# Running TensorE as two 64-row tiles in a two-problem attention kernel, with a planned load order

## The chip, the cores and the metric

The kernel runs on one core of a Trainium2 chip. The metric is the device time of one execution in microseconds (us), given as the median of several executions. A profiled execution comes with each kernel; its span differs from the median by a microsecond or two.

Engines in the profile: PE is TensorE's matmuls and PEld its weight loads, DVE is VectorE, ACT is ScalarE, POOL is GpSimd, SP is SyncE, which issues the DMAs.

## The reference

Two independent attention problems, A and B, of the same shape; the outputs are put side by side.

```python
B, Sq, D = 16, 144, 448
H, Sk, Dh = 16, 512, 256

def problem(x, k_cache, v_cache, wq, wo):            # all bf16
    q = (x @ wq).reshape(B, Sq, H, Dh).transpose(0, 2, 1, 3)
    scores = einsum("bhqd,bhkd->bhqk", q, k_cache) * Dh ** -0.5
    p = softmax(scores, axis=-1)
    o = einsum("bhqk,bhkd->bhqd", p, v_cache)
    return o.transpose(0, 2, 1, 3).reshape(B, Sq, H * Dh) @ wo

out = concatenate([problem(A...), problem(B...)], axis=-1)
```

A "unit" below is one (problem, batch, head), so there are 2 x 16 x 16 = 512. Each unit needs its own 512 x 256 K and V. For units 0 to 47 K is loaded as it lies and transposed on TensorE; from unit 48 on (464 units) the DMA transposes it. D is 448 = 3.5 x 128: this half is what the change is about.

## The kernel before

Per unit, PE does Q (8 matmuls with 128 contraction rows; the fourth chunk of D holds only 64 real rows and 64 zero rows), scores (8 matmuls of 144 columns), PV (8), a row sum (one matmul against a matrix of ones, for two units at a time), and on average 2.27 matmuls of 448 columns of the output projection. Q is done for two batches at once where it can be, in matmuls of 288 columns.

```python
wq_sb = sb("wq_sb", [128, 4, H * DH], BF16)      # fourth chunk: rows 0-63 set to zero
...
def t_q(U):
    ...
    def e(t):
        for dc in range(2):
            for kc in range(4):                  # 4 chunks of 128 rows: 3.5 are data
                c0 = h * DH + dc * 128
                acc = qp_ps[:, dc, 0:2 * SQ] if n == 2 else qp_ps[:, 0, dc * SQ:(dc + 1) * SQ]
                ins = t.matmul(acc, lhsT=wq_sb[:, kc, c0:c0 + 128],
                               rhs=xt_sb[:, kc, xo:xe + 1:max(xe - xo, 1), :], start=(kc == 0), stop=(kc == 3))
        return ins
...
def t_pv(U):
    ...
    ob = U % 2                                   # two PSUM banks for PV, by turns
    def e(t):
        for dc in range(2):
            for c in range(4):
                ins = t.matmul(ot_ps[ob][:, dc * SQ:(dc + 1) * SQ],
                               lhsT=v_sb[:, vsl, j, c * DH + dc * 128:c * DH + (dc + 1) * 128],
                               rhs=pt_sb[:, sl, c, :], start=(c == 0), stop=(c == 3))
        return ins
...
def t_halves(U):                                 # DVE: folds the exponentials' sums to 64 rows
    sl, p0 = U // 2 % NPS, U % 2 * 64            # two units share the 128 rows of one tile
    def e(v):
        return v.tensor_tensor(ps_sb[p0:p0 + 64, sl, :], p2_sb[0:64, :], p2_sb[64:128, :], op=ALU.add)
```

ACT takes the logarithm of the row sum and then exp(-log) for the reciprocal. DVE multiplies PV by it into a ring buffer (the "eviction") and, for every second unit, takes the maximum and minimum of the row sums; a flag computed from these selects a slow general path if a sum is out of bounds (it never is in these runs). The row sums start on POOL (`t_presum`), are folded on DVE (`t_halves`), and end in the matmul with ones.

The order of each engine's instructions is fixed when the kernel is built, and each engine runs them strictly in order:

```python
while True:
    ...
    for u in of_step(lq, i):
        if q_pair(u):
            t_q(u); t_evac_q(u)
    for u in of_step(ls, i):
        t_s(u)
    ...
    if P0 <= u < NT and u % 2:
        t_recip(u)
    if 0 <= u < NT:
        t_pv(u)
        if u < P0 or u % 2 == 0:
            t_sum(u)
    if P0 <= u + 2 < NT:
        t_halves(u + 2)                          # two units ahead
    ...
```

All eight PSUM banks are used: three for scores, two for Q, two for PV with the row sum, one for the projection. The loads follow two hand-written tables, one at the start and one at the switch from problem A to B.

## Time and profile before

| | before |
|---|---|
| median (2 runs) | 1055.65 us (1055.01 to 1056.3) |
| span of the profiled run | 1055.3 us |
| PV of unit 48 / of unit 511 begins | 126.4 us / 1045.1 us |
| PE busy | 98% |

The first view is the profile's page: span, busy times, the PE row of the 40 slices (busy tenths), the DMA queues (packets, MB, share of 16 engines), and the chain of work that ended last.

```profile
span 1055.3 us, 32320 instructions
PE 1031.0 (98%) x12376; PEld 875.0 (83%) x12376; DVE 740.9 (70%) x2039; ACT 793.9 (75%) x2365; POOL 636.6 (60%) x1030
...
PE   6999999999999999999999899999999999999997
...
q1 hardware_dynamic: 588896, 291.99, 110.9%
q8 instruction: 99, 1.62, 0.6%
...
PE 91%; DMA 5%; ACT 1%; DVE 1%; SPq 1%; issue 0%; POOL 0%; ACTq 0%; DVEq 0%
```

TensorE bounds the kernel: it is busy nearly throughout and is 91% of the chain. The line that looks like nothing is `q8 instruction`: 99 packets of 16 KB, the fetches of instructions. By the Trainium skill (cited below) one such packet is 256 instructions.

The timeline of PE near 500 us (start, us, engine, line, operation, count) shows that columns alone set the pace: eight matmuls of 144 columns begin every 0.50 us, 63 ns each, although one lasts about 230 ns.

```profile
500.05 0.66 PE L1142 MATMUL ot_ps<-pt_sb,v_sb 128*128 128x144 bf16 x8
500.55 0.23 PE L1158 MATMUL ot_ps<-ps_sb,ones 128*128 128x144 bf16 x1
500.61 0.54 PE L1259 MATMUL op_ps<-wo_sb,ring 128*128 128x448 bf16 x2
500.99 0.66 PE L1052 MATMUL qp_ps<-xt_sb,wq_sb 128*128 128x144 bf16 x8
501.49 0.66 PE L1086 MATMUL s_ps<-qt_sb,kt_sb 128*128 128x144 bf16 x8
```

The waits of PE (what it waited for: us in total, times, longest) are all small, and the two long ones after unit 48 are DMA waits at the switch from A to B.

```profile
PE s_ps L1000 <- DMA v_sb<-in_A_k_cache_dram: 6.3, 4, 4.7
PE qp_ps L1052 <- DMA wq_sb<-in_B_wq_dram: 3.6, 1, 3.6
PE s_ps L1086 <- DMA kt_sb<-in_B_k_cache_dram: 2.9, 1, 2.9
...
PE s_ps L1086 <- DVE qt_sb L1066: 1.5, 5, 0.4
```

The halving on DVE (busy us, mean ns, then idle before it):

```profile
L1120 DVE TENSOR_TENSOR ps_sb<-p_sb 64x144 bf16<-64x144 f32 x464 | 158.7, 342 | 44.4 <-POOL p_sb L1111 30.3
```

### The profile page before, as it was taken

The page shows a single profiled execution, that of the slowest core. Times are in us where ns is not written, and L with a number is a line of the kernel's source. Part 1 is how long each engine was busy: PE and PEld are TensorE (multiplying, and loading weights), DVE is VectorE, ACT ScalarE, POOL GpSimd, SP SyncE. Part 2 cuts the span into 40 slices and gives each one's busy share as a digit, 9 for nine tenths or more (in the row PEclk, how much of TensorE's full clock was granted, in tenths as well). Part 3 has the DMA queues.
Part 4 walks back from the last instruction along what each step waited for, and adds up shares of the span by engine and source line. Part 5 has one row for each costly group of instructions (what it writes and reads, how often), then busy time and mean ns, then how long its engine had stood idle before and what let it go on. Part 6 is the DMA issues. An engine that isn't in the chain of part 4 may idle for free.

```text
span 1055.3 us, 32320 instructions
## 1 busy us (share of the span) xinstructions
PE 1031.0 (98%) x12376; PEld 875.0 (83%) x12376; DVE 740.9 (70%) x2039; ACT 793.9 (75%) x2365; POOL 636.6 (60%) x1030
## 2 busy tenths in 40 slices
PE   6999999999999999999999899999999999999997
PEld 6999888888888888888878788888888888888885
DVE  4776666776766777777868667677776667777775
ACT  4887667777777777878857667777877777788785
POOL 3554556656666566666746556566666666666673
PEclk9999999999999999999999999999999999999999
DMA  9999999999999999999999999999999999999960
GB/s 316 372 343 291 294 291 248 283 299 271 264 305 260 248 286 262 304 289 280 283 281 343 279 283 287 303 284 292 251 279 280 278 286 298 296 254 274 292 201 14
DMA packets 589060, 294.15 MB, mean 279 GB/s; under 512 B 500832, under 2 KB 513632, under 8 KB 588896
## 3 DMA queue, kind: packets, MB, share of 16 engines
q1 hardware_dynamic: 588896, 291.99, 110.9%
q8 instruction: 99, 1.62, 0.6%
q14 instruction: 65, 0.53, 0.2%
HBM read 161.48 MB, written 4.13 MB: 157 GB/s over the span
## 4 chain that ended last, share of the span: by engine, by line
PE 91%; DMA 5%; ACT 1%; DVE 1%; SPq 1%; issue 0%; POOL 0%; ACTq 0%; DVEq 0%
PE s_ps L1086 23%; PE ot_ps L1142 23%; PE qp_ps L1052 22%; PE op_ps L1259 19%; DMA kt_sb<-in_B_k_cache_dram 2%; DMA v_sb<-in_A_k_cache_dram 2%; PE ot_ps L1158 2%; PE s_ps L1000 1%; PE qp_ps L1000 1%; DMA wq_sb<-in_B_wq_dram 1%; PE qp_ps L1259 1%; ACT rinv_sb L1179 0%; ACT pt_sb L1096 0%; DVE ring L1194 0%; DVE qt_sb L1066 0%
## 5 line engine op out<-in xcount | busy, mean ns | idle before, releaser
L1106 POOL TENSOR_TENSOR pp_sb<-pt_sb 128x288 f32<-128x288 bf16 x512 | 384.9, 752 | 322.5 <-ACT pt_sb L1096 308.1
L1096 ACT ACTIVATE pt_sb<-s_ps 128x288 bf16<-128x288 f32 x1024 | 364.6, 408 | 184.4 <-PE s_ps L1086 177.6
L1194 DVE TENSOR_TENSOR ring<-ot_ps,rinv_sb 128x288 bf16<-128x288 f32 (+2 forms) x640 | 241.9, 394 | 150.3 <-ACT rinv_sb L1179 145.8
L1086 PE MATMUL s_ps<-qt_sb,kt_sb 128*128 128x144 bf16 x4096 | 341.3, 226 | 4.7 <-DMA kt_sb<-in_B_k_cache_dram 2.9
L1142 PE MATMUL ot_ps<-pt_sb,v_sb 128*128 128x144 bf16 x4096 | 340.3, 226 | 0.0
L1086 PEld LDWEIGHTS s_ps<-qt_sb,kt_sb 128*128 128x128 bf16 x4096 | 287.7, 98 | 56.9 <-DVE qt_sb L1066 5.6
L1179 ACT ACTIVATE rinv_sb<-ln_sb 64x144 f32<-64x144 f32 x928 | 298.3, 321 | 24.3
L1052 PE MATMUL qp_ps<-xt_sb,wq_sb 128*128 128x288 bf16 (+1 forms) x2368 | 302.3, 271 | 6.6 <-DMA wq_sb<-in_B_wq_dram 3.6
L1259 PE MATMUL op_ps<-wo_sb,ring 128*128 128x448 bf16 x1120 | 285.2, 353 | 0.0
L1052 PEld LDWEIGHTS qp_ps<-xt_sb,wq_sb 128*128 128x128 bf16 x2368 | 212.3, 98 | 81.9 <-issue 7.5
L1142 PEld LDWEIGHTS ot_ps<-pt_sb,v_sb 128*128 128x128 bf16 x4096 | 274.5, 98 | 0.5
L1111 POOL TENSOR_TENSOR p_sb<-pp_sb 128x144 f32<-128x144 f32 x464 | 227.5, 490 | 74.6 <-DVE ps_sb L1120 10.4
L1209 DVE TENSOR_REDUCE run_sb<-ot_ps 128x1 bf16<-128x144 f32 x560 | 146.5, 304 | 79.4 <-ACT ln_sb L1166 44.3
L1120 DVE TENSOR_TENSOR ps_sb<-p_sb 64x144 bf16<-64x144 f32 x464 | 158.7, 342 | 44.4 <-POOL p_sb L1111 30.3
L1066 DVE CAST qt_sb<-qp_ps 128x576 bf16<-128x576 f32 x216 | 162.1, 751 | 21.3 <-PE qp_ps L1052 17.7
L1259 PEld LDWEIGHTS op_ps<-wo_sb,ring 128*128 128x128 bf16 x1120 | 94.0, 98 | 21.2
L1166 ACT ACTIVATE ln_sb<-ot_ps 128x144 f32<-128x144 f32 x232 | 67.9, 293 | 32.6 <-PE ot_ps L1158 25.3
L1158 PE MATMUL ot_ps<-ps_sb,ones 128*128 128x144 bf16 x280 | 63.4, 226 | 0.0
L1065 DVE CAST qt_sb<-qp_ps 128x288 bf16<-128x288 f32 x80 | 35.9, 448 | 4.8 <-PE qp_ps L1052 4.3
L1008 ACT ACTIVATE kt_sb<-qp_ps 128x512 bf16<-128x512 bf16 x48 | 28.9, 603 | 7.3 <-PE qp_ps L1000 7.3
L1111 POOL TENSOR_TENSOR ps_sb<-pp_sb 128x144 bf16<-128x144 f32 x48 | 23.5, 490 | 6.9 <-PE ot_ps L1158 0.3
L1158 PEld LDWEIGHTS ot_ps<-ps_sb,ones 128*128 128x128 bf16 x280 | 27.5, 98 | 0.0
(29 smaller groups left out, 153.4 us busy)
## 6 DMA issues: line engine op xcount, KB each, us to landing
v_sb<-in_A_v_cache_dram SPq DMA_DIRECT2D x128, 512.0 KB, 7.1
v_sb<-in_B_v_cache_dram SPq DMA_DIRECT2D x128, 512.0 KB, 7.5
v_sb<-in_A_k_cache_dram SPq DMA_DIRECT2D x24, 512.0 KB, 9.6
out_dram<-ost_sb SPq DMA_DIRECT2D x36, 112.0 KB, 6.2
wo_sb<-in_A_wo_dram SPq DMA_DIRECT2D x8, 448.0 KB, 8.7
wo_sb<-in_B_wo_dram SPq DMA_DIRECT2D x8, 448.0 KB, 9.0
wq_sb<-in_A_wq_dram SPq DMA_DIRECT2D x4, 768.0 KB, 10.1
wq_sb<-in_B_wq_dram SPq DMA_DIRECT2D x4, 768.0 KB, 10.6
```

Of the source, the lines that this page charges most:

```text
L1052: ins = t.matmul(acc, lhsT=wq_sb[:, kc, c0:c0 + 128], rhs=xt_sb[:, kc, xo:xe + 1:max(xe - xo, 1), :], start=(kc == 0), stop=(kc == 3))
L1066: return v.tensor_copy(qt_sb[:, a:b + 1:b - a, :, :], qp_ps[:, :, 0:2 * SQ].rearrange("p e (u q) -> p u e q", u=2))
L1086: ins = t.matmul(s_ps[bank][:, (c % 2) * SQ:(c % 2 + 1) * SQ], lhsT=kt_sb[:, 2 * c + dc, ko:ko + 128], rhs=qt_sb[:, qsl, dc, :], start=(dc ...
L1096: return a.activation(pt_sb[:, psl, 2 * k:2 * k + 2, :].rearrange("p b q -> p (b q)"), s_ps[bank][:, 0:2 * SQ], AF.Exp, scale=DH ** -0.5)
L1106: return g.tensor_tensor(pp_sb[:, :, :], pt_sb[:, psl, 0:2, :], pt_sb[:, psl, 2:4, :], op=ALU.add)
L1111: return g.tensor_tensor(dst, pp_sb[:, 0, :], pp_sb[:, 1, :], op=ALU.add)
L1120: return v.tensor_tensor(ps_sb[p0:p0 + 64, sl, :], p2_sb[0:64, :], p2_sb[64:128, :], op=ALU.add)
L1142: ins = t.matmul(ot_ps[ob][:, dc * SQ:(dc + 1) * SQ], lhsT=v_sb[:, vsl, j, c * DH + dc * 128:c * DH + (dc + 1) * 128], rhs=pt_sb[:, sl, c, ...
L1179: return a.activation(rinv_sb[p0:p0 + 64, sl, :], ln_sb[h0:h0 + 64, :], AF.Exp, scale=-1.0)
L1194: ins = v.tensor_tensor(ring[:, 2 * h:2 * h + 2, r0:r0 + q1 - q0], ot_ps[ob][:, 0:2 * SQ].rearrange("p (c q) -> p c q", c=2)[:, :, q0:q1], ...
L1209: return v.tensor_reduce(run_sb[:, k, j:j + 1], ot_ps[ob][:, 2 * SQ:3 * SQ], axis=AX.X, op=op)
L1259: ins = t.matmul(acc[0:m, 0:D], lhsT=ring[:, c, col0:col0 + m], rhs=wo_sb[:, c, :], start=(c == first), stop=(c == last))
```

## The change

The intent: since 448 = 7 x 64, Q needs only seven half-chunks of contraction instead of eight. If PE is used as two tiles of 64 rows that run side by side, every matmul becomes two halves with half the rows each, both adding into the same PSUM bank, and Q's two output halves need 7 half-matmuls each, 14 in place of 16. That removes one eighth of Q. Two tiles may not write one bank at once (the prediction names the page that says so), so the upper tile runs one group behind the lower.

With it come: an extra copy of x's last 64 rows to the other half of the partitions (DVE); the row sum as one half-matmul per unit (before: one whole one per two units); log and reciprocal done whole for each unit on ACT; the max and min checks replaced by running sums that the halving and the reciprocal write on the side; deeper buffers for Q (13 for 11) and for the partial row sums (2 for 1); and a planner that orders the loads from estimated times. The diff, cut to its core:

```diff
+    def tiles(self, lo, hi, after=None, clear=(), rank=1, **kw):
+        own = set(kw["banks"]) | set(clear)
+        ...                                       # upper groups on the same banks go first
+        self._put(PL, lo, self._ready((lo, after, kw)), **kw)      # lower tile now
+        self.late.append((hi, after, kw, self.step, rank))         # upper tile later
+        while self.late:
+            k, first = self._next()
+            if first > self.now[PL]:
+                break
+            self._pop(k)
...
-        wq_sb = sb("wq_sb", [128, 4, H * DH], BF16)
+        wq_sb = sb("wq_sb", [128, 3, H * DH], BF16)
+        wr_sb = sb("wr_sb", [128, H * 128], BF16)                  # last 64 rows, one half per dc
...
+        def q_tiles(U, dc):
+            ...
+            def tile(p):                          # p is LO (rows 0-63) or HI (64-127)
+                ms = [mm(acc, wq_sb[p, kc, c0:c0 + 128], xt_sb[p, kc, xsl, :], n * SQ, p is LO and kc == 0)
+                      for kc in range(3)]
+                if (p is HI) == (dc == 1):        # the seventh half-chunk goes to one tile
+                    ms.append(mm(acc, wr_sb[p, h * 128:(h + 1) * 128], xt_sb[p, 3, xsl, :], n * SQ))
+                return ms
...
+        def pv_tiles(U, after):
+            ...
+            def tile(p):
+                ms = [mm(ot_ps[ob][:, dc * SQ:(dc + 1) * SQ], v_sb[p, ...], pt_sb[p, sl, c, :], SQ, ...)
+                      for dc in range(2) for c in range(4)]
+                if (p is HI) == (U % 2 == 1):     # the row sum, on one tile
+                    ms.append(mm(ot_ps[ob][:, 2 * SQ:3 * SQ], ones[p, :], ps_sb[p, ss, :], SQ))
+                return ms
...
-                return v.tensor_tensor(ps_sb[p0:p0 + 64, sl, :], p2_sb[0:64, :], p2_sb[64:128, :], op=ALU.add)
+                    return v.scalar_tensor_tensor(ps_sb[p0:p0 + 64, sl, :], p2_sb[0:64, U % 2, :], 1.0,
+                                                  p2_sb[64:128, U % 2, :], op0=ALU.mult, op1=ALU.add,
+                                                  accum_out=big_sb[p0:p0 + 64, n:n + 1])
...
+                    return a.activation(rinv_sb[:, sl, :], rinv_sb[:, sl, :], AF.Exp, scale=-1.0,
+                                        accum_out=small_sb[:, U:U + 1])
...
-    START = ("n0 q0 x0 n1 v0 n2 q1 v1 ...")       # tables of loads
-    MID = ("k16 v127 v128 q0 ...")
+        while todo:                               # planner: the first load that may start goes next
+            for m in todo:
+                ...
+                start = max(now, at(lo) if lo > s_min else now)
+                if best is None or start < best[0]:
+                    best = (start, m, lo)
+            ...
...
+            if P0 <= i < NT:
+                if qus:
+                    q_tiles(qus[0], 0)
+                ...
+                if more:
+                    s_tiles(i + ls(NT), 0)
+                if is_split(i):
+                    project(i, True)
+                if i + 1 < NT:
+                    t_halves(i + 1)               # one unit ahead; before: two
+                ...
+                pv_tiles(i, lambda u=i: finish_unit(u, u))
```

## The prediction

> **What bounds it now.** TensorE. The page gives PE 98% busy, and the chain of waits that ended last is 91% PE (scores 23%, PV 23%, Q 22%, output projection 19%). Start to start, the timeline shows a 144-column matmul about every 63 ns, 288 columns every 123, 448 every 189: columns/2.4 GHz plus 2.5 ns, as the Trainium skill states ("TensorE: Matmul & The Clock Gate", "Wait — 56ns, not 53.3ns?"). So weight loads are hidden and only streamed columns count. Per unit after unit 48: scores 0.504, PV 0.504, Q 8 x 61.5 ns = 0.49, row sum 0.03, projection 2.27 x 189 ns = 0.43; sum 1.96 us. Measured from unit 48 (126.4 us) to unit 511 (1045.1): 1.984, of which two DMA waits at the switch from A to B (526 and 601 us, about 7 us together) are 0.015.
>
> Around that: 16 us until the first PV, 10 us after the last.
>
> DMA is a close second: busy at 9 tenths or more in nearly all slices. In the second half it never runs empty; K (16 units) takes 17 to 18 us of queue time and a two-unit V about 1.45 to 1.5, so 16 units with stores and x need about 30.3 us, 1.89 us a unit (estimate from the DMA issues and bytes moved).
>
> **The change.** Two 64-row tiles halve a matmul's rows but not its columns, so scores, PV and projection stream as long as before if both tiles run concurrently. The gain is Q: 448 = 7 x 64, so 7 half-chunks share two tiles and 1/8 of Q goes: 61.5 ns x 464 units = 28.5 us, all on the critical path. The row sum costs the same. Units before 48 stream the same.
>
> Off the path: the max and min checks (304 ns each on DVE) mostly go; two half exponentials (2 x 321 ns) become one; DVE about 1.2 us a unit, ACT about 1.55, both under 1.9.
>
> PE and LDWEIGHTS instructions double to about four per 63 ns. This trace cannot show that tiles overlap; the skill says they "can execute LdWeights and Matmul in parallel" ("TensorEngine Tiling (Array Packing)", "Key Properties"). "Gotcha 1: PSUM Pressure" there forbids two row tiles in one bank at once; hence the lag.
>
> New pitch 1.90 us, against DMA's 1.89: the slack that absorbed B's weights (about 20 us extra) shrinks. I expect 10 to 15 us of DMA waits around the switch (before 7), and a few us of pipeline gaps.
>
> Sum: 1055.6 - 28.5 + 5 (DMA) + 2 (gaps) - 3 (planner, tail) = **1031 us**, range **1014 to 1058**. Chances: faster by over 2% 0.55, within 2% 0.37, slower 0.08.
>
> **What would show it.** Right: about twice as many matmuls and loads; same-tile 144-column starts 63 ns apart with the other tile's between them; pitch near 1.90; PE waits on K or weights around units 256 to 305; DMA saturated throughout. The min and max reduces gone from DVE.
>
> **What would make it wrong.** If the two tiles' weight loads or issues serialise, a pair of halves takes over 63 ns and all of it is on the path: 5 ns a pair, at about 23 pairs a unit, costs 53 us. If DMA sustains less than 1.90 us a unit, the gain is swallowed by K and V waits. If in-order waits block both tiles, PE gaps appear at group starts. If the planner removes the switch and start waits, it ends near 1015.

## The result

The kernel after takes 1157.95 us (median of 2 runs, 1157.51 to 1158.4). The ratio after over before is 1.0975 (95% interval 1.0943 to 1.1007): slower by almost 10%.

The page of the kernel after, the same lines:

```profile
span 1156.7 us, 52423 instructions
PE 1047.9 (91%) x22468; PEld 968.6 (84%) x22468; DVE 716.7 (62%) x2034; ACT 734.0 (63%) x2645; POOL 624.2 (54%) x1030
...
PE   7999899989989999998779889999899999899997
...
q1 hardware_dynamic: 592608, 291.99, 104.0%
q8 instruction: 178, 2.92, 1.0%
...
PE 71%; DVE 11%; ACT 9%; issue 6%; DMA 1%; SPq 1%; POOL 0%; DVEq 0%; POOLq 0%
```

Three things changed in the chain: PE fell from 91% to 71%, DVE and ACT rose from 2% to 20%, and "issue" came up with 6%, time in which PE waited for nothing that the profile shows. The DMA share fell to 1%, and the loads moved the same 291.99 MB.

The timeline of PE shows the tiles working as meant, and then a hole. The first lines alternate between scores on one tile and PV on the other, about 10 to 20 ns apart, each with its own pitch of about 63 ns:

```profile
329.18 0.22 PE L1779 MATMUL s_ps<-qt_sb,kt_sb 64*128 64x144 bf16 x1
329.19 0.22 PE L1779 MATMUL ot_ps<-pt_sb,v_sb 64*128 64x144 bf16 x1
329.24 0.22 PE L1779 MATMUL s_ps<-qt_sb,kt_sb 64*128 64x144 bf16 x1
329.25 0.22 PE L1779 MATMUL ot_ps<-pt_sb,v_sb 64*128 64x144 bf16 x1
...
329.38 0.22 PE L1779 MATMUL ot_ps<-pt_sb,v_sb 64*128 64x144 bf16 x1
329.43 0.35 PE L1779 MATMUL op_ps<-wo_sb,ring 64*128 64x448 bf16 x1
331.22 0.23 PE L1779 MATMUL ot_ps<-ps_sb,ones 64*128 64x144 bf16 x1 [1.45 <-issue]
```

Nothing was waited for at 331.22 that the profile knows of, and both tiles stood still. The waits of the kernel after have such lines in number, beside waits on DVE and ACT:

```profile
...
DVE ring L1411 <- ACT rinv_sb L1394: 341.8, 441, 3.5
...
PEld ot_ps L1779 <- issue: 28.8, 29, 2.3
...
PEld ot_ps L1779 <- DVE ps_sb L1322: 24.3, 49, 1.0
PE ot_ps L1779 <- issue: 23.9, 28, 1.5
PEld s_ps L1779 <- issue: 17.5, 18, 1.9
...
PE ot_ps L1779 <- DVE ps_sb L1322: 14.0, 35, 0.7
PE s_ps L1779 <- issue: 13.4, 14, 2.1
```

(A PEld wait and a PE wait can be the same time seen twice, so these are not to be added.)

### Where the 101 us went

To split the difference, each tile matmul of the trace was matched with the kernel's program. The "work" of a tile is its streamed columns at 2.4 GHz plus 2.6 ns per matmul; a stall is a start that comes more than 20 ns after the tile was free and the instruction before it was issued, and it is put down to what that instruction waits for. All for the stretch from the PV of unit 48 to the PV of unit 508, where only the new scheme runs (our own table, not a view of the profile; us):

```
                              before    after
length of the stretch          912.6   1004.1
work of one tile / of the array 898.7    869.8
stalls at a page border           0       72.3   (77 times)
waits on DVE or ACT             ~4.5     ~60     (halving 25.8, Q's copies to SBUF 18.5,
                                                   exponentials 7.8, copies of x 7.3)
DMA waits                        6.8       0
```

The few us that the table leaves over lie for the most part in stretches of 3.4 us at half the clock, by the trace's clock record: two in the kernel before, each just after one of its two DMA waits (3.4 us lost), and one in the kernel after (1.7 us).

So the change delivered what it promised in work, 898.7 - 869.8 = 28.9 us, and then lost 72 us in one place and some 55 in another. Outside the stretch it loses 1.6 us before the first PV, 4.5 in units 0 to 48 and 3.6 at the end. (28.9 less, 120.4 more inside, 9.7 outside: 101.2; the spans differ by 101.4.)

### What a page border is

The 72 us are all in one kind of place. Counting PE's instructions (matmuls, weight loads, semaphore waits) in order, every gap over 0.3 us that has no semaphore to explain it, 69 of them with 73.9 us in sum, stands at the same place modulo 256: instruction 193 of 256. Every other residue has 3 us or less. 256 instructions are one 16 KB packet of the queue `q8 instruction`, and the Trainium skill says just this: instructions are "refilled in 16 KiB blocks", and the next block is fetched while the present one runs ("Runtime: NRT & Kernel Launch", "Instruction fetch mechanics"). The trace agrees with the block size.

The times of those packets complete the picture (from the trace's DMA records and our count of instructions):

- A block lasted 10.8 us before (median), because 256 instructions were some 125 matmuls of the whole array (12,376 over 99 packets). With twice as many instructions for the same columns it lasts 6.1 us after (5.2 at the least). This counts the stalls themselves; in `a_noload` below, which has the same instructions and no such stalls, it is 5.7.
- The request for the next block goes out when PE crosses into the present one, or shortly after (in `a_noload` the packet itself begins 0.4 us after the crossing, in the median). From the crossing to the first byte of the packet it took 2.4 us before and 3.4 us after (4.0 where the transposing K loads run), the packet takes about 0.9 to 1.1 us, and PE goes on 1.2 to 1.6 us after it landed. In the hole shown above, the packet began at 328.7 us, landed at about 329.6, and PE resumed at 331.22.
- So a block is there about 4.7 us after the request before, against a life of 10.8: no stall. In the kernel after it is there 5.5 to 6.7 us after the request, against a life of about 5.7 without stalls: PE often runs dry. (Estimates: sums of the measured pieces, with PE's delay after the landing, which only shows where PE ran dry, taken from the kernel after.)

### What the waits on DVE and ACT are

Two changes in the trace go with the other 55 us. First, each result takes longer to finish, because its lower half runs first and its upper half later, interleaved with other groups: from the first to the last matmul of a PV it took 0.50 us before and 1.54 after (medians), of a Q pair 0.98 and 2.61, of a unit's scores 0.50 and 2.55. The result keeps its PSUM bank all that time, and there are no more banks than before. Second, DVE and ACT carry the running sums:

```profile
L1322 DVE SCALAR_TENSOR_TENSOR ps_sb<-p_sb 64x144 bf16<-64x144 f32 x464 | 236.9, 511 | 15.4 <-POOL p_sb L1311 0.8
...
L1394 ACT ACTIVATION_READ_ACCUMULATOR rinv_sb<-rinv_sb 128x1 bf16 x512 | 96.6, 189 | 0.0
...
L1322 DVE DVE_READ_ACCUMULATOR ps_sb<-p_sb 64x1 bf16 x464 | 37.2, 80 | 0.0
```

The halving takes 511 ns in the mean against 342 before, not because of its form (both have a fastest of 303 ns) but because it meets POOL: 223 of 464 are over 0.5 us (39 before). The skill says that a "DVE instruction with two SBUF inputs contends with a GpSimd instruction that reads SBUF" ("SBUF — State Buffer", "Who interferes with whom"); the trace agrees, with a detail: what counts is who begins first. The long ones take 0.74 us in the median, and 220 of the 223 (all 39 before) begin while POOL's addition of 288 columns is under way; a halving that begins first stays at 0.31 us (some 310 times in the kernel before, though such an addition began during it).

The timeline of DVE shows how one wait arises. DVE stands idle for the reciprocal of one unit, then evicts, then halves (slowly, at 0.74 us); PE needs this halving for the row sum that ends a PV group, and the group's first matmul waits 0.31 us for it, until 347.04:

```profile
345.74 0.46 DVE L1411 TENSOR_TENSOR ring<-ot_ps,rinv_sb 128x288 bf16<-128x288 f32 x1 [0.50 <-ACT rinv_sb L1394]
346.23 0.74 DVE L1322 SCALAR_TENSOR_TENSOR ps_sb<-p_sb 64x144 bf16<-64x144 f32 x1
346.90 0.08 DVE L1322 DVE_READ_ACCUMULATOR ps_sb<-p_sb 64x1 bf16 x1
```

```profile
346.44 0.29 PE L1779 MATMUL s_ps<-qt_sb,kt_sb 64*128 64x144 bf16 x3
347.04 0.23 PE L1779 MATMUL ot_ps<-pt_sb,v_sb 64*128 64x144 bf16 x1 [0.31 <-DVE ps_sb L1322]
```

DVE is busy only 62% of the span, and still it holds PE up, since it works in strict order and is idle at the wrong times.

### The profile page after: what moved, and what is told of

Same layout as the page of the kernel before. It is cut to its first block, busy times and chain, and to the rows that moved or that the text cites. A ratio compares the mean times of both kernels' runs of the same rounds, so it can differ in the third digit from the quotient of the medians.

```text
span 1156.7 us, 52423 instructions
## 1 busy us (share of the span) xinstructions
PE 1047.9 (91%) x22468; PEld 968.6 (84%) x22468; DVE 716.7 (62%) x2034; ACT 734.0 (63%) x2645; POOL 624.2 (54%) x1030
## 3 DMA queue, kind: packets, MB, share of 16 engines
q1 hardware_dynamic: 592608, 291.99, 104.0%
## 4 chain that ended last, share of the span: by engine, by line
PE 71%; DVE 11%; ACT 9%; issue 6%; DMA 1%; SPq 1%; POOL 0%; DVEq 0%; POOLq 0%
PE ot_ps L1779 21%; PE s_ps L1779 17%; PE qp_ps L1779 14%; PE op_ps L1779 11%; ACT rinv_sb L1394 4%; DVE ps_sb L1322 4%; DVE ring L1411 4%; ACT rinv_sb L1388 3%; PE s_ps L1259 2%; PE ot_ps L1347 2%; PE qp_ps L1180 2%; DVE qt_sb L1239 1%; ACT pt_sb L1276 1%; DVE xt_sb L1136 1%; PE op_ps L1483 1%
## 5 line engine op out<-in xcount | busy, mean ns | idle before, releaser
L1779 PE MATMUL s_ps<-qt_sb,kt_sb 64*128 64x144 bf16 x7376 | 624.2, 223 | 18.4 <-issue 13.4
L1779 PE MATMUL ot_ps<-pt_sb,v_sb 64*128 64x144 bf16 x7424 | 548.4, 223 | 34.4 <-issue 18.4
L1779 PE MATMUL op_ps<-wo_sb,ring 64*128 64x448 bf16 x2104 | 529.4, 350 | 5.3 <-issue 5.2
L1779 PEld LDWEIGHTS s_ps<-qt_sb,kt_sb 64*128 64x128 bf16 x7376 | 479.4, 94 | 37.7 <-issue 17.5
L1779 PEld LDWEIGHTS ot_ps<-pt_sb,v_sb 64*128 64x128 bf16 x7424 | 444.6, 94 | 55.0 <-DVE ps_sb L1322 24.3
L1779 PE MATMUL qp_ps<-xt_sb,wq_sb 64*128 64x288 bf16 (+1 forms) x2904 | 440.3, 276 | 24.6 <-DVE qt_sb L1236 7.4
L1779 PEld LDWEIGHTS qp_ps<-xt_sb,wq_sb 64*128 64x128 bf16 x2904 | 230.3, 94 | 47.9 <-issue 10.6
L1322 DVE SCALAR_TENSOR_TENSOR ps_sb<-p_sb 64x144 bf16<-64x144 f32 x464 | 236.9, 511 | 15.4 <-POOL p_sb L1311 0.8
L1779 PEld LDWEIGHTS op_ps<-wo_sb,ring 64*128 64x128 bf16 x2104 | 172.3, 94 | 6.7 <-issue 6.3
L1394 ACT ACTIVATE rinv_sb<-rinv_sb 128x144 f32<-128x144 f32 x512 | 165.3, 323 | 16.2
L1394 ACT ACTIVATION_READ_ACCUMULATOR rinv_sb<-rinv_sb 128x1 bf16 x512 | 96.6, 189 | 0.0
L1779 PEld LDWEIGHTS ot_ps<-ps_sb,ones 64*128 64x128 bf16 x464 | 43.6, 94 | 4.9 <-issue 4.9
L1322 DVE DVE_READ_ACCUMULATOR ps_sb<-p_sb 64x1 bf16 x464 | 37.2, 80 | 0.0
```

The costliest lines, as they stand in the source:

```text
L1322: return v.scalar_tensor_tensor(ps_sb[p0:p0 + 64, sl, :], p2_sb[0:64, U % 2, :], 1.0, p2_sb[64:128, U % 2, :], op0=ALU.mult, op1=ALU.add, ...
L1394: return a.activation(rinv_sb[:, sl, :], rinv_sb[:, sl, :], AF.Exp, scale=-1.0, accum_out=small_sb[:, U:U + 1])
L1779: ins_ = eng.matmul(w["out"], lhsT=w["lhsT"], rhs=w["rhs"], start=w["start"], stop=last, skip_group_check=True)
```

## The experiments

Two theories for the larger loss:

- **Pages**: the doubled number of instructions shortens the life of an instruction page, and its fetch, queued among the K and V loads, comes too late.
- **Tiles** (rival): the two tiles hinder each other (weight loads or issue serialise, or a drain when they change groups), and the border is a coincidence.

And for the smaller: **late results** (each result spans two groups, on the same banks, with DVE and ACT in strict order) against **extra work** (the running sums and reads of accumulators lengthen DVE's and ACT's loops) and **order** (the halving only stands in the wrong place of DVE's order).

Sixteen kernels ran. Those with wrong results are named so; their times are of use because nothing in the program depends on the values except the flag, and the general path did not run (`a_noload` has the same 52,423 instructions as the kernel after, `b_split_noload` the same 56,304 as `b_split`).

### a_noload and b_noload: almost no K and V traffic, in both kernels

K and V loads past the first ring of buffers are cut to 16 rows of 64 elements; every DMA and wait stays. Results are wrong.

```diff
+                if W >= 5:
+                    a = sl * KW * 128
+                    return q.dma_start(kt_sb[0:16, 0, a:a + 64], src[0:16, 0:64]).then_inc(sems["kt%d" % sl], 16)
...
+                if v_seq["v", G] >= NV:
+                    return q.dma_start(v_sb[0:16, sl, 0, 0:64], src[0:16, 0, 0:64]).then_inc(sems["v%d" % sl], 16)
```

> The kernel after, with K and V loaded only until every buffer has been filled once and then replaced by 2 KB loads (wrong results on purpose). The trace of after shows PE idle for 73.9 us in 69 gaps of over 0.3 us that all begin at the same place of every 256 PE instructions, and 16 KB instruction packets landing about 1.3 us before each gap ends. Theory F (instruction pages of 256 instructions queue behind the K and V traffic): with the traffic gone these gaps fall under 15 us and the time falls to 1070 to 1095 us; the waits on VectorE and ScalarE, about 60 us, stay. Rival (a page is slow to come whatever the DMA engines do): the gaps stay at 60 to 80 us and the time stays above 1135.

> Control: the same removal of K and V traffic in the kernel before (wrong results on purpose). It has no gaps at page borders, so only its DMA waits go (about 7 us at the switch from A to B and some at the start): 1035 to 1052 us under every theory. If it gains as much as a_noload does, the traffic costs TensorE in some other way than by instruction pages.

Measured: `a_noload` 1095.16 us (ratio to before 1.0375, 1.0358 to 1.0392), `b_noload` 1045.67 us (0.9908, 0.9892 to 0.9925). In the stretch the page-border stalls go from 72.3 to 0, with all tile instructions still there and 178 instruction packets as in the kernel after. A packet now begins 0.4 us after the border instead of 3.4. The kernel before gains 10 us from the same cut: its DMA waits (6.8) and the half clock after them (3.4). Waits on DVE and ACT stay, even grow from about 60 to 70.7 us (perhaps because the page stalls had given DVE and ACT time to catch up). From its page (all the instruction packets are still there; the 2% of "issue" are the start and pieces too short for the list of waits), and the two main lines of its waits, in which no matmul waits on issue:

```profile
q8 instruction: 178, 2.92, 1.1%
...
PE 71%; DVE 14%; ACT 10%; issue 2%; SPq 1%; DMA 1%; POOL 0%; DVEq 0%; POOLq 0%
```

```profile
PEld ot_ps L1784 <- DVE ps_sb L1327: 30.3, 57, 1.0
PE ot_ps L1784 <- DVE ps_sb L1327: 18.7, 43, 0.7
```

What follows: the stall at the border needs the load traffic. The tiles alone do not cause it. The other loss does not need the traffic. That `a_noload` still ends 49 us behind `b_noload` shows that the change as a whole loses even with free loads.

### b_split and b_split_noload: the doubled instructions without the tiles

In the kernel before every matmul except the transposes is issued as two matmuls of half the columns, on the whole array.

```diff
+                n = out.shape[-1] // 2
+                ...
+                self.whole(out[:, 0:n], lhsT=lhsT, rhs=parts[0], **kw)
+                return self.whole(out[:, n:2 * n], lhsT=lhsT, rhs=parts[1], **kw)
```

> The kernel before, still one 128-row array, with every matmul but the transposes cut into two of half the columns (72, 144 or 224), each with its own weight load: about 24,000 matmuls and 48,000 PE instructions, a little more than after has, and no tiles. Columns streamed are the same; 2.5 ns more a matmul gives 30 us, so 1085 us if nothing else happens. Theory F: a page of 256 instructions then lasts about 5.5 us, and gaps at one place of every 256 instructions appear, 50 to 100 us in sum; time 1120 to 1190. Rival (tiles are at fault): no gaps at page borders, 1075 to 1095. If half-width pairs are bound by the weight load instead, same-line starts spread evenly to 45 ns or more and the time is above 1250 with few gaps.

> b_split (one array, twice the matmuls, 1183 us, 108 us of gaps at page borders) without the K and V traffic; wrong results as in b_split. Theory F: the gaps at page borders go and 1065 to 1085 us remain. Rival (so many matmuls are slow in themselves): above 1150.

Measured: `b_split` 1183.12 us (1.1193, 1.1152 to 1.1234), `b_split_noload` 1083.37 us (1.0259, 1.0234 to 1.0284). The gaps over 0.3 us of `b_split` are again all at residue 193: 87 gaps, 108.0 us. Without the traffic 9 gaps with 10.7 us are left, all in the first 150 us, where the first loads still run in full; on its page "issue" is 1% of the chain. The page and the timeline of `b_split`:

```profile
q8 instruction: 193, 3.16, 1.1%
...
PE 89%; issue 8%; ACT 1%; DVE 1%; DMA 0%; SPq 0%; POOL 0%; ACTq 0%; DVEq 0%
```

```profile
360.49 0.20 PE L1497 MATMUL s_ps<-qt_sb,kt_sb 128*128 128x72 bf16 x1
360.52 0.20 PE L1496 MATMUL s_ps<-qt_sb,kt_sb 128*128 128x72 bf16 x1
362.95 0.19 PE L1497 MATMUL s_ps<-qt_sb,kt_sb 128*128 128x72 bf16 x1 [2.24 <-issue]
```

The half matmuls themselves have the expected pitch (33 ns for 72 columns, 63 for 144, 96 for 224). The results of `b_split` came out wrong (relative error 0.363), which was not intended. The likely reason, which no run tests: a start flag on the second half of a bank makes the accumulation of the first half begin anew, as the skill describes for the zero region of a whole 2 KiB bank ("PSUM — Partial Sum Buffer", "The four PSUM rules"). The instructions, bytes and waits are the same, so the timing stands.

What follows: the page stall is reproduced with one array and no tile at all. The rival falls for this part.

### b_nop2: empty instructions to shorten the pages (inconclusive)

```diff
+                for _ in range(2):
+                    self.eng.nop(nofuse=True)
+                return self.eng.matmul(*a, **kw)
```

> The kernel before, still in one 128-row array, with two empty sequencer instructions put before each matmul, so that PE fetches about 49,000 instructions instead of 24,900, as after does. Theory F: gaps at one place of every 256 instructions appear, 50 to 100 us in sum, and the time rises to 1105 to 1165. Rival (it is the two tiles, not the count of instructions): no such gaps and a time within 15 us of before, unless the empty instructions themselves hold the sequencer, which would show as time spread evenly over all matmuls and not at one place.

Measured: 1063.77 us (1.0083, 1.0062 to 1.0104), results right. But the trace has only 105 instruction packets, so the empty instructions were not in the program as fetched instructions (1,746 of them appear as semaphore waits at their line). The run did not test the theory, which is why `b_split` was made.

### a_kw4: K in loads of 4 units instead of 16

If the fetch waits behind the long K transfers, shorter ones might let it through.

```diff
-    KW, KR = 16, 32
+    KW, KR = 4, 32
...                                               # the planner's estimate of one K load scaled alike
```

> The kernel after with K loaded 4 units at a time instead of 16, the planner otherwise the same: K and V alternate finely. In after an instruction page begins to arrive 4.0 us (median) after the previous border while K transposes run and 2.4 us otherwise; with a page life of 5.5 us and about 2.3 us from there to running, only the K stretches are late. Theory F: mixing makes the delay about 3.2 us throughout, page gaps fall from 73.9 to 20 to 45 us, time 1105 to 1140. If the transposes lose speed in small pieces, DMA waits appear instead and the time is above 1160.

Measured: 1215.98 us (1.1505, 1.1467 to 1.1544), results right. The expectation was missed: page stalls rose from 72.3 to 120.8 us (97 times), and another 29 us of stalls were put down to no wait. The trace's clock record can account for most of these: this run's granted clock was 0.983, with 12 stretches of 3.4 us at half the clock inside the kernel, 20 us lost (41 us at half). Each begins between 0.2 us before and 1.4 us after the end of a page stall of 1.8 to 3.4 us, so a long stall can cost more than itself; not every long stall has such a stretch behind it (2.3 us at 674 us in the kernel after has none, 2.1 us at 182 us has one). Smaller K transfers are thus not a way out. The skill says that a DMA engine takes turns between queues packet by packet and finishes a packet first ("DMA: Bandwidth & Descriptors", "Queues, rings and completion order"). That fits the delay of 3.4 us with loads and 0.4 without, but no run here looks at the turns themselves.

### b_plan: the planner alone

The kernel before with the planner in place of its tables (with 1.97 us a unit as its estimate).

```diff
-    START = ("n0 q0 x0 n1 v0 ...")
-    MID = ("k16 v127 v128 q0 ...")
+        while todo:
+            ...
```

> The kernel before with the load planner of the change in place of the two written-out load orders, nothing else (unit pitch in the planner 1.97 us instead of 1.91). My prediction gave the planner and the tail 3 us: 1045 to 1054. b_noload (1045.7) is the floor for anything that only orders loads. If the planner is one of the costs of after, it is above 1060.

Measured: 1059.77 us (1.0033, 1.0016 to 1.005), results right; between the two expectations. In the stretch DMA waits are 10.3 us against 6.8. In the old kernel the planner costs about 3 us; it is not where the 101 us went.

### b_q7: the seventh half-chunk in the kernel before

Only Q's remainder on two 64-row tiles: six whole matmuls, then two half ones.

```diff
-            for dc in range(2):
-                for kc in range(4):
+            for kc in range(3):
+                for dc in range(2):
                     ...
+            for dc in range(2):
+                p = slice(64 * dc, 64 * dc + 64)
+                ins = t.matmul(qp_ps[:, dc, 0:2 * SQ], lhsT=wr[p], rhs=xt_sb[p, 3, xs_, :], start=False, stop=True)
```

> The kernel before with only Q in seven half-chunks: in one array, three whole chunks and then the two remainders of a pair as two 64-row matmuls side by side. This streams 1/8 less of Q (28.5 us) with fewer matmuls, but each pair goes from whole array to tiles and back. In after, before unit 48, two such groups took 1.06 us against 0.984 for eight whole matmuls: if each of the 232 pairs does so, the time rises by 10 to 22 us, to 1066 to 1078. If the switches are hidden, it falls to about 1028.

Measured: 1125.75 us (1.0648, 1.062 to 1.0675), results right. Two losses: PE waits 43.6 us for the copies of x's last rows, which this version puts late into DVE's order (a fault of the experiment), and going from whole array to tiles and back. From the last whole matmul to the first half one it takes 218 ns start to start, and back 225, against 123 for matmuls of this width: 95 and 102 ns lost, against 123 ns saved per pair. In total a Q pair takes 1.060 us (median) against 0.984 for eight whole matmuls; over 232 pairs that is 18 us, as expected, and the copies make the expectation miss. The skill says that a change of tiling mode drains TensorE ("TensorEngine Tiling (Array Packing)", "Key Properties"); the trace agrees.

```profile
501.75 0.91 PE L1093 MATMUL qp_ps<-xt_sb,wq_sb 128*128 128x288 bf16 x6 [1.17 <-DVE xt_sb L1049]
502.59 0.30 PE L1099 MATMUL qp_ps<-xt_sb,wr_sb 64*128 64x288 bf16 x2
502.82 0.55 PE L1133 MATMUL s_ps<-qt_sb,kt_sb 128*128 128x144 bf16 x6
```

What follows: the saving cannot be had by tiling only Q's remainder in this way.

### a_noacc, a_noload_noacc: without the running sums

The halving and the reciprocal no longer write running sums (the checks then look at zeros; results are right in `a_noacc`).

```diff
-                    return v.scalar_tensor_tensor(ps_sb[p0:p0 + 64, sl, :], p2_sb[0:64, U % 2, :], 1.0,
-                                                  p2_sb[64:128, U % 2, :], op0=ALU.mult, op1=ALU.add,
-                                                  accum_out=big_sb[p0:p0 + 64, n:n + 1])
+                return v.tensor_tensor(ps_sb[p0:p0 + 64, sl, :], p2_sb[0:64, U % 2, :],
+                                       p2_sb[64:128, U % 2, :], op=ALU.add)
```

> The same edit in after with its traffic. If waits on engines and page gaps simply add, the time falls by as much as in a_noload_noacc, to 1115 to 1140. If the page supply holds PE (as a_halves2 suggests: there the wait on the halving vanished and page gaps and other waits grew), the page gaps grow by most of what is gained and the time stays within 1140 to 1160.

> a_noload (no K and V traffic, wrong results on purpose), and the two running sums that the change added are taken out: the halving is a plain addition again and the reciprocal exponential sums nothing. Theory D: these sums cost 189 ns on ScalarE and about 250 ns on VectorE in the loop PV, logarithm, exponential, eviction, halving, PV; without them PE's wait on the halving (31.8 us in a_noload) falls under 12 us and the time falls from 1095 to between 1050 and 1075. Rival (the loop is too long even without them): less than 10 us is gained.

Measured: `a_noacc` 1150.09 us (1.0896, 1.0858 to 1.0933), 8 us better than the kernel after; `a_noload_noacc` 1080.29 us (1.0224, 1.0193 to 1.0255; wrong), 15 us better than `a_noload` (5 us above what theory D expected). Waits on DVE and ACT in the stretch: about 47 us in `a_noacc` (after: about 60) and 57.3 in `a_noload_noacc` (`a_noload`: 70.7). Extra work is a part of the loss, 13 us of these waits, but most remains without it. The page stalls took little of the gain back (about 3 us more in `a_noacc`).

### a_halves2 and a_noload_noacc_h2: the halving a unit earlier in DVE's order

The halving for unit i + 2 behind the PV of unit i, as in the kernel before, instead of unit i + 1 ahead of it.

```diff
-                if i + 1 < NT:
-                    t_halves(i + 1)
...
                 A.settle()
+                if i + 2 < NT:
+                    t_halves(i + 2)
```

> The kernel after, with the halving addition of a unit (VectorE) emitted a unit earlier, so that it no longer stands in VectorE's order behind the eviction of the unit two before. Theory D (a loop PV, logarithm, reciprocal, eviction, halving, PV holds PE because the halving now takes 0.31 or 0.74 us): PE's wait on it (25.8 us in 93 waits at PV) falls under 8 us and the time falls by 15 to 35 us, to 1122 to 1143; the page gaps stay. Rival (these waits are only an echo of the page gaps): the time changes by less than 8 us.

> a_noload_noacc (no K and V traffic, no running sums, 1080 us; wrong results on purpose) with the halving emitted a unit earlier as in a_halves2. PE still waits 25.5 us on the halving and 30 us on Q's evictions, x copies and exponentials. If the loop over the halving is what is left of the first, its wait goes and the time falls to 1050 to 1068. If the other waits take its place, as in a_halves2 with traffic, it stays at 1075 or more.

Measured: `a_halves2` 1169.42 us (1.1078, 1.1059 to 1.1096; right), `a_noload_noacc_h2` 1084.52 us (1.0266, 1.0249 to 1.0283; wrong). The wait on the halving is gone in both (25.8 us to 0), but in its place come waits on the copies of x (17.4 and 22.4 us) and Q's copies to SBUF (28.6 and 29.5). With all other things equal (`a_noload_noacc`) the sum of waits goes from 57.3 to 60.4 us. With traffic the page stalls grew too, by some 15 us (a simpler count of the trace gives 84 us for `a_halves2` and 69 for the kernel after), which fits its being 11 us slower; neither expectation with traffic foresaw that. The order alone is not the cause: a wait moved, none was removed.

### a_noload_late2, a_noload_noacc_late2, a_noacc_late2: the eviction later in DVE's order

The eviction of a unit is put off to the start of the step two units on, so that DVE need not stand waiting for the reciprocal.

```diff
+                while ot_due and ot_due[0] <= i - 2:
+                    t_evac_ot(ot_due.pop(0))
```

> a_noload (no K and V traffic, running sums kept, 1095 us, wrong results on purpose) with one thing moved: the eviction of a unit (VectorE) is emitted a step later, so that in VectorE's order the halving and the eviction of Q come before it and not behind it. Theory H (head of line: VectorE stands waiting for ScalarE's reciprocal, and everything PE needs is behind it): PE's 70 us of waits on VectorE and ScalarE fall under 40 and the time falls by 25 to 50 us, to 1045 to 1070. Rival (VectorE is simply late in every order, as the two earlier moves suggest): within 10 us of 1095.

> The same move on top of a_noload_noacc (1080 us, PE waits 57 us on other engines). Theory H: under 30 us of waits, 1035 to 1055, which is below the kernel before and shows the 28 us of Q. Rival: within 10 us of 1080.

> The same two edits with all traffic (correct results; a_noacc was 1150). If page supply and engine waits add: 1105 to 1125. If pages take back most of what is freed, as in a_halves2: 1125 to 1150, with page gaps of 85 us or more. Either way it is above the 1056 of before, since the pages alone cost over 70.

Measured: 1237.3 us (1.1704), 1232.1 us (1.1651; both wrong) and 1248.21 us (1.1809; right): every expectation was missed by over 90 us. In `a_noload_noacc_late2` 196.8 us (205 times) are waits of PV on the eviction: PV has two banks, each held from its first lower half to its eviction, so a late eviction blocks the next PV. The idle time of DVE before the eviction cannot simply be filled; with two PV banks the eviction must be prompt. All eight banks are used, so a third one for PV would have to come from another stage; that was not tried.

### a_whole: everything in the change but the tiles

The kernel after with each pair of halves joined into one whole matmul: planner, order, running sums, copies stay. The row sum is then a full matmul per unit (before: one per two units), and the seventh half-chunk is added in a way that is not exact; the difference was within the comparison's tolerance, but it must not be used as it is.

```diff
     def tiles(self, lo, hi, after=None, clear=(), rank=1, **kw):
+        def e(t):
+            for k, w in enumerate(lo):
+                ins = t.matmul(w["out"], lhsT=w["lhsT"], rhs=w["rhs"], start=w["start"], stop=k == len(lo) - 1, ...)
+            return ins
+        self.whole(e, sum(self.cost(lo)), **kw)
...
-        LO, HI = slice(0, 64), slice(64, 128)
+        LO, HI = slice(0, 128), slice(64, 128)
```

> All of the change except the tiles: every pair of half matmuls of after is issued as one 128-row matmul at the place of its lower half, with no lag, so Q takes eight half-chunks again, as in before; planner, running sums, leads and orders stay those of after. (Q's eighth matmul multiplies a remainder that belongs to the other half, so the results are wrong on purpose; shapes and durations are those of a right one.) If the tiles cause both halves of the loss, page gaps by the count of instructions (then 25,000 again) and waits on VectorE by the later results (in after a unit's PV takes 1.54 us from first to last matmul, in before 0.50), both vanish: page gaps under 5 us, engine waits under 20 us, time 1045 to 1065. If the running sums, the planner or the orders carry the engine waits, 40 us or more of them stay and the time is above 1085.

Measured: 1078.88 us (1.0207, 1.0181 to 1.0233; 5 rounds; slower, but whether by 2% is unclear). The expectation was missed by 14 us at its upper end; the term that was forgotten is the full row sum: work in the stretch is 912.1 us against 898.7 before, 13.4 us more. No page stalls, and waits on DVE and ACT of about 7 us, against 60 in the kernel after. From the first to the last matmul PV takes 0.56 us, close to before. The halving is as slow as in the kernel after (510 ns in the mean). The page:

```profile
span 1077.1 us, 32597 instructions
...
q8 instruction: 101, 1.65, 0.6%
...
PE 94%; ACT 2%; DVE 1%; DMA 1%; SPq 1%; issue 0%; POOL 0%; DVEq 0%; POOLq 0%
```

What follows: with the same DVE and ACT instructions (accumulator reads and all) in nearly the same order, taking the tiles away takes away both losses. For the second loss there is a catch: without tiles PE has 42.3 us more work in the stretch (912.1 against 869.8), and a slower PE alone leaves DVE and ACT more time. But less its DMA waits of 8.4 us the stretch of `a_whole` lasts 920.8 us, against 941.0 in `a_noload` (both read from the traces). So DVE and ACT can get through the stretch 20 us faster than they did for the tiles in `a_noload`: at least 20 of its 70.7 us of waits come with the tiles, and the extra work by itself does not make these. The rest may be the tiles or may be PE's shorter work meeting the same loops; no run here has the short work without the tiles. That the tiles act through the lateness of the results and the banks they hold is the reading that fits all runs; the runs show the split, not the lag by itself.

## Why the prediction was wrong, point by point

- **"TensorE bounds it; columns count; Q's saving is 28.5 us, all on the critical path."** Right in size: the work of the stretch fell by 28.9 us (898.7 to 869.8).
- **Tiles overlap; about twice as many matmuls; 144-column starts 63 ns apart with the other tile's between them.** Right: 22,468 matmuls against 12,376, 63 ns in the median, the other tile's start between them (10 to 20 ns later in the lines shown). The worry named first, that loads or issues of the two tiles serialise, did not come true.
- **"+2 (gaps)", "a few us of pipeline gaps".** This is the step that failed. All stalls in the stretch went from about 14 us (of which 7 DMA) to 134 us. Of these 72 us are page borders and some 60 us waits on DVE and ACT.
  - The prediction had seen that "PE and LDWEIGHTS instructions double", and took the cost only as issue time. It did not ask how instructions reach the engine. The trace of before showed the numbers: 99 instruction packets, a block in 10.8 us, 2.4 us to its packet. The life of a block halved, about 5.4 us, against 3.3 us for delay and packet and a restart of unknown length on top, would have left little margin. The delay then grew too, from 2.4 to 3.4 us (3.5 in `b_split`), and none was left. `a_noload` takes the stall away without touching an instruction of PE, and `b_split` makes it in a kernel without tiles: this cause is shown.
  - "DVE about 1.2 us a unit, ACT about 1.55, both under 1.9", hence off the path. The busy times were not far off (in the 1004.1 us and 460 units of the stretch DVE was busy for 632.3 us, 1.37 a unit, with its accumulator reads and the contention, and ACT for 637.8, 1.39), but busy time is not the test. Our reading is that a strict order and two or three banks per stage make latency count, and latency per result rose about threefold (PV) to fivefold (scores). What is shown is less: these waits go when the tiles go (`a_whole`), at least 20 us of them because of the tiles, and 13 us go with the running sums (`a_noacc`; the two may overlap).
- **"+5 (DMA): 10 to 15 us of waits around the switch".** Wrong in sign: none in the stretch, since the kernel after is slower than its loads. Nothing is learnt of what a faster one would have met. In the stretch no load held PE up by coming late; the loads held it up by standing in the way of the instruction fetch. The floor for the old kernel with almost no loads is 1045.67 us (`b_noload`).
- **"-3 (planner, tail)".** Wrong: the planner alone is +3 us (`b_plan`), and the kernel after loses 1.6 us at the start, 4.5 in units 0 to 48 and 3.6 at the end.
- **"If in-order waits block both tiles, PE gaps appear at group starts"** was listed as a risk and came true, but was given no weight in the sum or the range.

What stays open: how the 60 us divide between the lag of the upper tile, the number of PSUM banks, DVE's strict order, and the mere fact that PE has less work per unit. We think that these go together (the lag hurts because there are few banks, and the order matters because the lag leaves no slack), but no run changed the lag or the banks alone. Why smaller K loads made the page stalls worse is also open, and so is why the delay of a packet grew with twice the instructions although the loads moved more slowly (255 GB/s in the mean against 279). No version with full traffic and right results beats the kernel before; the nearest, `b_plan`, is the same within 2% and slower by 0.3%.

## What to carry to other kernels

Count instructions as bytes that must be fetched: divide 256 by the instructions per microsecond of the busiest engine, and compare this life of a block with the time from one border to the arrival of the next packet under your own DMA load, which the trace of the old kernel shows (here 2.4 us of delay and 0.9 of transfer, and over a microsecond until PE goes on, of a life of 10.8 us, which the change halved). Leave a margin: here the delay itself grew to 3.4 us. When a change splits a result into parts that finish at different times, ask for its latency and the buffers that it holds, not for the busy time of the engines behind it. To tell such causes apart, take away the traffic and keep the instructions, and double the instructions without the new scheme. When you take the scheme away, as in `a_whole`, look whether the bounding engine's own work stayed the same; if it did not, the waits that vanish are not all the scheme's.

## What the Trainium skill lacked or had wrong

- "Runtime: NRT & Kernel Launch", "Instruction fetch mechanics", says "The cost of crossing a 16 KiB boundary is one DMA tail-bump, mostly hidden." Here 77 borders cost 72.3 us (0.94 us each) with two tiles, and 87 cost 108.0 us with one array and half-width matmuls, when the DMA queues are full of loads; with almost no loads the cost is 0. The page does not say that the fetch queues with the loads (2.4 to 4.0 us until its packet begins, 0.4 without them), nor give the life of a block that is needed.
- The same page gives PE a buffer of 2048 instructions in one sentence and speaks of only two blocks, without excepting PE, in another. The trace has one block ahead: the request for a block follows the border into the one before it, and PE runs dry one block later.
- "TensorEngine Tiling (Array Packing)", "Key Properties", says that a change of mode drains TensorE but has no number: here 95 ns into 64-row tiles and 102 ns back, more than the 123 ns that one saved matmul of 288 columns is worth. It also does not say that tiles run half-matmuls at twice the instruction rate, so that the fetch above becomes the limit.
- No page has the latency side of row tiles: with the second tile a group behind, a PV result takes 1.54 us from its first to its last matmul against 0.50, and a bank is held that much longer.
- "VectorE: DVE Perf Modes" says that an operation with an accumulator output is two instructions, but not what the second costs, and "ScalarE: Activation LUTs" names the accumulator output without a second instruction: here the read takes 80 ns on DVE and 189 ns on ACT each time, 37.2 and 96.6 us in all.
